# Other places for the weight loads of the slot experts in a fused convolution and expert kernel

## The chip, the core and the metric

The kernel runs on one core of a Trainium2 chip. The core has a matrix engine (TensorE, PE in the rows; PEld is its loading of the stationary operand), a vector engine (VectorE, DVE), a scalar engine (ScalarE, ACT), a general engine (GpSimd, POOL) and a sequencer that issues most transfers (SyncE, SP). Sixteen DMA engines move data between memory and the core's on-chip buffers. The metric is the device time in microseconds (us), as the median of several runs.

## What is computed

```python
# _attn_ref: softmax over 7 taps per head, then a causal 7-tap convolution whose weights differ by row and head
w = np.exp(weight_gen - weight_gen.max(-1)); w /= w.sum(-1)          # [4, 3584, 8, 7]
out = np.einsum('bshk,bskhg->bshg', w, x_unf)                        # x: [4, 3584, 192]
# _moe_ref: soft slots, 8 experts x 4 slots
logits = x @ phi                                                     # [14336, 32]
slot_input = softmax(logits, over rows).T @ x                        # [32, 192]
for e in range(8):
    slot_out[e] = np.maximum(slot_input[e] @ w1[e], 0.0) @ w2[e]     # w1 [192, 1024], w2 [1024, 192]
x = softmax(logits, over slots) @ slot_out
# _moe2_ref: each row goes to its best of 8 experts, scaled by two gates
...
```

The change concerns the weights `w1` and `w2` of `_moe_ref`, here called the slot experts' weights.

## The kernel before

The first stage, some 177 of 280 us, runs over 32 groups `g` of 112 rows in each of the 4 sequences. For each group SP loads rows of the input (`load_x`, line 318, tile x: one large and two small transfers) and normalised tap weights (`load_v`, line 300, tile vt: the same three), and VectorE (quarters q = 0 and 2) and GpSimd (q = 1 and 3) make banded matrices from vt (`band`, line 331). TensorE multiplies x by the bands (`conv`, line 352, into psA and psB), computes the slot logits (line 369) and turns the result (line 383); ScalarE copies between. A running softmax over the rows adds up the slot inputs (lines 393 to 454).

The tap weights pass through a softmax of their own, in six blocks: load (`w_load`, line 148, tile wg), maximum (line 157), subtraction, exponential, sum, normalisation (`w_rot`, line 209, tile vr), and a store to scratch memory vscr (`w_store`, line 214), out of which `load_v` reads. Blocks 0 to 2 are done in the prologue; block 3 is loaded there and finished in groups 1 to 4, block 4 runs in groups 2 to 11, block 5 in 9 to 20. So the vt load of a group waits for the store of its block.

The slot experts' weights are 24 transfers, three for each expert e: 512 KB of `w1` (w1a, line 277), the remaining 256 KB of `w1` (w1b, line 279) and 768 KB of `w2` (w2s, line 281). They have buffers of their own, so nothing has to be free first. Loop g of the groups 1 to 24 issues number g - 1, in the order expert by expert. Below, a0 is w1a of expert 0, b0 its w1b, w0 its w2s. They are used only after the groups: w1a and w1b in lines 787 and 789, w2s in line 803 (first four f blocks of experts 0 to 3, then of experts 4 to 7, then the other four).

SP issues all of these from one queue in the order of the program, and where a transfer has to wait, all behind it wait. Each transfer uses one of eight completion semaphores in turn, so that it also waits for the landing of the transfer eight places earlier. x has three buffers, so the x load in loop g (for group g + 2) waits for the matmuls of group g - 1; vt has four buffers.

After the groups a second softmax, over the slots, runs in four chunks on VectorE, ScalarE and GpSimd; its result is stored to scratch memory cscr (line 561) and loaded back turned (`load_c`, line 565, tile cT; two transfers a chunk). Chunks 0 and 1 are stored during the groups and loaded right after them; chunks 2 and 3 follow beside the slot experts. Their output (so, line 819) picks one expert, whose weights SP then loads (lines 842 and 844, tiles w1t and w2t). The last stage, from about 220 us, writes the output.

Of the kernel before, what the change touches and what calls it, by code (L numbers as in the profile page):

```python
# [57 lines left out]
def dram_ap(t, off, dims):  # L58
    return bass.AP(t.tensor, t.offset + off, [list(d) for d in dims])
# [3 lines left out]
def attn_moe_moe_kernel(ctx: ExitStack, tc: tile.TileContext, x, wgen, phi, mw1, mw2, w_gate, w_ogate, w1, w2, out, dbg=None):  # L63
# [147 lines left out]
    def w_store(i):  # L211
        rt, t0 = RTS[i], T0S[i]
        vr = pcs.pop(i)[2].rearrange("p t h k -> p (t h k)")
        nc.sync.dma_start(dram_ap(vscr, (t0 + PAD) * HK, [[rt * HK, 32], [SROW * HK, B], [1, rt * HK]]), vr[:, 0 : rt * HK])
# [19 lines left out]
    for v, i in ((mask_s[:, 0:BT], -PAD), (mask_s[0:HI, BT:], -PAD), (mask_s[HI:P, BT:], 0), (mask_h[HI:P], -HI)):  # L234
        n = v.shape[-1]
# [37 lines left out]
    def load_moe(i):  # L273
        e, k = divmod(i, 3)
        r0 = 64 * (e // 4)
        if k == 0:
            nc.sync.dma_start(w1a[:, e, :], mw1[e, 0:P, :])
        elif k == 1:
            nc.sync.dma_start(w1b[r0 : r0 + 64, e % 4, :], mw1[e, P:D, :])
        else:  # L280
            nc.sync.dma_start(w2s[:, e], mw2[e].rearrange("(c p) d -> p c d", p=P))


    vts, xts, bts, pss, aTs, ats, Ls, dTs, lps = {}, {}, {}, {}, {}, {}, {}, {}, {}
# [12 lines left out]
    def load_v(g):  # L297
        vts[g] = p2.tile([P, B, HK], F32, tag="vt", name=f"vt_{g}", bufs=4)
        for p, t, n, b in rows(g):
            nc.sync.dma_start(vts[g][p : p + n, b:], dram_ap(vscr, (b * SROW + g * BT + t + PAD) * HK, [[HK, n], [SROW * HK, B - b], [1, HK]]))  # L300
# [302 lines left out]
    w_rot(0, range(0, 6))  # L603
    w_rot(0, range(6, K), nc.gpsimd)
    w_store(0)
    nc.scalar.dma_start(dram_ap(vscr, 0, [[HK, PAD], [SROW * HK, B], [1, HK]]), zrow.unsqueeze(1).to_broadcast([PAD, B, HK]))
    load_v(0)
    load_v(1)
# [6 lines left out]
    def store_1():  # L615
        w_store(1)
        load_phi(4, H)
        load_v(2)
        load_v(3)
        w_load(3)  # L620

    start = dict(
        phi=lambda: load_phi(0, 4),
# [10 lines left out]
        st1=store_1,  # L634
# [11 lines left out]
            start[f"b{g}{q}"] = lambda g=g, q=q: band(g, q)  # L646
    for n in PRO.split():
        start[n]()
    if PS[3][1] < 0:
        w_max(3, 0, RH // 2)  # L650

# [4 lines left out]
    def do_steps(t):  # L656
        for f, a in wsteps.pop(t, []):
            f(*a)

    for g in range(NG):  # L660
        m, hf = divmod(g, 2)
        if 2 < g + 2 < NG:
            load_x(g + 2)
        if 3 < g + 3 < NG:
            load_v(g + 3)
        if 1 <= g <= NG:
            conv_out(g - 1)
        if SM and hf == 1 and m >= 1:
            soft_m(m - 1)
        last = g + 1 == NG or g == 0  # L670
        if not last:
            band(g + 1, 0)
            band(g + 1, 3)

        if hf == 1 and m >= 1:
            if not SM:
                soft_m(m - 1)
            soft_2(m - 1)

        if hf == 0 and m >= 2:  # L680
            soft_p(m - 2)
            soft_a(m - 2)
        conv(g, 0)
        conv(g, 1)
        if hf == 0 and m >= 1:
            scores(m - 1)
            soft_0(m - 1)
        conv(g, 2)
        conv(g, 3)
        xts.pop(g)  # L690
        if not last:
            band(g + 1, 1)
        do_steps(3 * g)
        if g >= 1:
            if hf == 1 and m >= 1 and g < NG - 1:
                soft_t(m - 1)
                soft_d(m - 1)
            turn(g - 1, 0)
            turn(g - 1, 1)
        if not last:  # L700
            band(g + 1, 2)
        if hf == 0 and m >= 1:
            soft_1(m - 1)
        do_steps(3 * g + 1)
        if 1 <= g <= 24:
            load_moe(g - 1)
        if g == 2:
            nc.sync.dma_start(wgt[:, :, 0:E], w_gate.rearrange("(c p) e -> p c e", p=HC))
            nc.sync.dma_start(wgt[:, :, E : 2 * E], w_ogate.rearrange("(c p) e -> p c e", p=HC))
        if g == 20:  # L710
            wstack.close()
            cstack = ctx.enter_context(ExitStack())
            cpl = pool(cstack, "pcs", 2, "right")
            nc.vector.tensor_tensor(sel, ident[:, 0:32], ident[:, 32:64], op=ALU.add)
            nc.vector.tensor_tensor(sel, sel, ident[:, 64:96], op=ALU.add)
            nc.vector.tensor_tensor(sel, sel, ident[:, 96:128], op=ALU.add)
            nc.vector.tensor_copy(sel4, sel.unsqueeze(1).to_broadcast([P, 4, NS]))

            wm = cpool.tile([HC, 1], F32, tag="wm", name="wm")
            nc.vector.tensor_reduce(wm, wgt.rearrange("p c e -> p (c e)"), axis=AX.X, op=ALU.max, apply_absolute_value=True)  # L720
            nc.gpsimd.affine_select(tri, ones1, pattern=[[1, P]], compare_op=ALU.is_ge, fill=0.0, base=0, channel_multiplier=-1)
        do_steps(3 * g + 2)
    if dbg is not None:
        nc.sync.dma_start(dbg["acc"], acc)
    tail()
    s1.close()


# [208 lines left out]
    g16 = fp.tile([P, NT, 2 * E + 1], F32, tag="g16", name="g16")  # L937
# [371 lines left out]
    def kappa():  # L1309
# [5 lines left out]
        a0=lambda: g_out(0), a1=lambda: g_out(1), t0=lambda: g_turn(0), t1=lambda: g_turn(1),  # L1315
# [121 lines left out]
```

## Time and profile before

| | |
|---|---|
| time, median of 3 runs | 283.66 us (283.58 to 284.75) |
| profiled execution, its own time | 281.31 us |
| its span, first to last instruction | 279.5 us |
| granted TensorE clock, mean | 0.939 |
| busy: PE, DVE, ACT, POOL | 75%, 72%, 55%, 52% of the span |
| moved by DMA | 54.79 MB, 196 GB/s mean |
| chain that ended last, by engine | PE 40%, DMA 27%, DVE 10%, issue 7%, ACT 6% |
| in it, largest single line | DMA x<-in_x_dram 14% |

Busy time is an average over stages with different limits, so it is read by stretches. The chain follows the work that ended last back from the end: at each step to what released it, or to the instruction before it on the same engine. "issue" is time in which an engine waited for nothing that the profile shows. The DMA share of a stretch is the mean share of time in which the sixteen DMA engines were busy. The clock of a stretch is given as a share of full speed (2.4 GHz; the lower level, 1.2 GHz, is 0.5).

### The profile page before, as it was taken

The page shows a single profiled execution, that of the slowest core. Times are in us where ns is not written, and L with a number is a line of the kernel's source. Part 1 is how long each engine was busy: PE and PEld are TensorE (multiplying, and loading weights), DVE is VectorE, ACT ScalarE, POOL GpSimd, SP SyncE. Part 2 cuts the span into 40 slices and gives each one's busy share as a digit, 9 for nine tenths or more (in the row PEclk, how much of TensorE's full clock was granted, in tenths as well). Part 3 has the DMA queues.
Part 4 walks back from the last instruction along what each step waited for, and adds up shares of the span by engine and source line. Part 5 has one row for each costly group of instructions (what it writes and reads, how often), then busy time and mean ns, then how long its engine had stood idle before and what let it go on. Part 6 is the DMA issues. An engine that isn't in the chain of part 4 may idle for free.

```text
span 279.5 us, 12314 instructions
## 1 busy us (share of the span) xinstructions
PE 210.7 (75%) x5188; PEld 168.7 (60%) x5188; DVE 200.0 (72%) x458; ACT 152.6 (55%) x408; POOL 146.1 (52%) x161
## 2 busy tenths in 40 slices
PE   0035496987878779695988789999869899999850
PEld 0034375765757566574767567736747688988750
DVE  2998899645797439569495486387857897988760
ACT  2112273463755576452658567626314598889750
POOL 8174695795728867484677798425202040513000
PEclk9999688698999999997999999999986999999995
DMA  6825689999898989796998871375599067667780
GB/s 202 180 64 178 207 225 272 274 225 234 222 280 258 228 213 255 178 234 177 264 262 207 219 166 54 72 161 116 135 276 198 7 203 243 220 192 232 226 268 17
DMA packets 64809, 54.79 MB, mean 196 GB/s; under 512 B 20399, under 2 KB 61227, under 8 KB 64747
## 3 DMA queue, kind: packets, MB, share of 16 engines
q1 hardware_dynamic: 64707, 53.92, 72.4%
q8 instruction: 43, 0.70, 1.1%
q14 instruction: 19, 0.16, 0.2%
q10 hardware_dynamic: 40, 0.01, 0.0%
HBM read 37.85 MB, written 16.06 MB: 193 GB/s over the span
## 4 chain that ended last, share of the span: by engine, by line
PE 40%; DMA 27%; DVE 10%; issue 7%; ACT 6%; SPq 1%; DVEq 0%; ACTq 0%
DMA x<-in_x_dram 14%; PE tp L383 7%; PE psA L352 7%; PE psB L352 5%; DMA out_dram<-ot 3%; DMA w2t<-in_moe_w_dram 3%; PE op L1382 3%; PE L L369 3%; DMA w2s<-in_moe_w_dram 2%; PE sp L444 2%; PE op L1385 2%; PE op L1384 2%; PE op L1383 2%; DMA vt<-vscr 2%; DMA vscr<-vr 2%
## 5 line engine op out<-in xcount | busy, mean ns | idle before, releaser
L331 POOL TENSOR_TENSOR bt<-vt,mask_s 128x448 f32<-128x448 f32 (+1 forms) x63 | 95.2, 1537 | 41.0 <-DMA vt<-vscr 27.3
L352 PE MATMUL psA<-bt,x 64*32 64x56 f32 (+1 forms) x1568 | 54.3, 246 | 27.9 <-issue 13.1
L331 DVE TENSOR_TENSOR bt<-vt,vbank 128x448 f32<-128x448 f32 x65 | 53.2, 832 | 28.1 <-DMA vt<-vscr 16.1
L352 PEld LDWEIGHTS psA<-bt,x 64*32 64x32 f32 (+1 forms) x1568 | 36.2, 114 | 41.0 <-issue 21.8
L352 PE MATMUL psB<-bt,x 64*32 64x56 f32 (+1 forms) x1568 | 54.7, 245 | 5.5 <-issue 5.5
L387 ACT ACTIVATE at<-tp 112x384 f32<-112x384 f32 x62 | 29.8, 492 | 28.2 <-PE tp L383 27.1
L383 PE MATMUL tp<-ident,aT 128*112 128x128 f32 x256 | 39.6, 291 | 1.4 <-DVE acc L454 0.9
L352 PEld LDWEIGHTS psB<-bt,x 64*32 64x32 f32 (+1 forms) x1568 | 36.7, 114 | 6.3 <-issue 6.3
L383 PEld LDWEIGHTS tp<-ident,aT 128*112 128x112 f32 x256 | 29.4, 141 | 6.4 <-ACT d L432 3.6
L1387 ACT ACTIVATE ot<-op,S 128x192 f32<-128x192 f32 x77 | 29.1, 431 | 5.0 <-DMA out_dram<-ot 1.7
L1382 PE MATMUL op<-wm,hi 128*128 128x192 f16 x112 | 27.5, 245 | 3.3 <-ACT ot L1387 1.9
L1385 PE MATMUL op<-Ml,cT 128*128 128x192 f16 x112 | 27.5, 246 | 0.2 <-DVE Ml L1306 0.2
L1383 PE MATMUL op<-wm,lo 128*128 128x192 f16 x112 | 27.5, 246 | 0.1
L1384 PE MATMUL op<-wm,hi 128*128 128x192 f16 x112 | 27.5, 246 | 0.1
L1076 DVE SCALAR_TENSOR_TENSOR lo<-hp,hi 128x512 f16<-128x512 f32 x28 | 19.1, 681 | 2.7 <-ACT hi L1075 2.6
L168 ACT ACTIVATE wg<-wg 128x952 f32<-128x952 f32 (+3 forms) x11 | 9.0, 829 | 19.8 <-DVE wg L164 9.0
L357 ACT ACTIVATE aT<-psA 128x224 f32<-128x224 f32 (+1 forms) x60 | 18.4, 361 | 1.5 <-PE psA L352 1.5
L357 ACT ACTIVATE aT<-psB 128x224 f32<-128x224 f32 (+1 forms) x60 | 19.0, 380 | 0.0
L1075 ACT ACTIVATE hi<-hp 128x512 f16<-128x512 f32 x28 | 16.8, 600 | 3.7 <-PE hp L1074 3.6
L369 PE MATMUL L<-aT,phi_p 128*32 128x112 f32 x512 | 17.0, 268 | 0.9 <-issue 0.6
L164 POOL TENSOR_TENSOR wg<-wg,mx 128x952 f32<-128x952 f32 (+3 forms) x9 | 13.6, 1527 | 6.0 <-DVE mx L157 6.0
L1383 PEld LDWEIGHTS <-lo 128*128 128x128 f16 x112 | 10.9, 97 | 8.1 <-DVE ot L1389 1.9
(265 smaller groups left out, 394.7 us busy)
## 6 DMA issues: line engine op xcount, KB each, us to landing
x<-in_x_dram SPq DMA_DIRECT2D x32, 336.0 KB
w2s<-in_moe_w_dram SPq DMA_DIRECT2D x8, 768.0 KB
out_dram<-ot SPq DMA_DIRECT2D x15, 384.0 KB
w1a<-in_moe_w_dram SPq DMA_DIRECT2D x8, 512.0 KB
cT<-cscr SPq DMA_DIRECT2D x8, 448.0 KB
vt<-vscr SPq DMA_DIRECT2D x32, 98.0 KB
out_dram<-ot SPq DMA_DIRECT2D x9, 288.0 KB
vscr<-vr SPq DMA_DIRECT2D x3, 784.0 KB
```

What stands on the lines that cost most here:

```text
L331: (nc.gpsimd if onp else nc.vector).tensor_tensor(bt.rearrange("p h (r k) -> p h r k", k=K), vt.unsqueeze(2).to_broadcast([n, H, w // K, K ...
L352: nc.tensor.matmul(out, xt[p, q * D + GR * h : q * D + GR * h + 32], bt[p, h, :], start=True, stop=True, tile_position=(HI * (r or 0), o))
L357: act = lambda o, i: nc.scalar.activation(o, i, AF.Copy)
L369: nc.tensor.matmul(Ls[m][32 * b : 32 * b + 32, o], phi_p[:, c, :], aTs[2 * m + q][:, c, b * BT : (b + 1) * BT], start=(c == 0), stop=(c == ...
L383: nc.tensor.transpose(tp[:, q, c, :], aTs[g][:, c, o : o + BT], ident)
L387: nc.scalar.activation(o, i, AF.Copy)
L1076: low = lambda: nc.vector.scalar_tensor_tensor(lo[:, f, :], hp, 0.0, hi[:, f, :], op0=ALU.max, op1=ALU.subtract)
L1382: nc.tensor.matmul(op, hi[:, 0, tok], wm2[:, 0, :], start=True, stop=False)
L1383: nc.tensor.matmul(op, lo[:, 0, tok], wm2[:, 0, :], start=False, stop=False)
L1384: nc.tensor.matmul(op, hi[:, 0, tok], wm2[:, 1, :], start=False, stop=False)
L1385: nc.tensor.matmul(op, cT[:, t * P : (t + 1) * P], Ml, start=False, stop=True)
L1387: nc.scalar.activation(ot[:, j, :], op, AF.Copy, scale=S0[:, t : t + 1])
```

## The change

The loop's `load_moe(g - 1)` goes, and a table names the place of each of the 24 transfers. Six go into the prologue: a0 behind the store of block 0, a1 behind the first four phi loads, and a2, b0, b1, a3 behind the load of block 3. The other w1 parts stand two or three loops apart. w0, w1 and w2 are issued in loops 19, 22 and 25, and w3 to w7 in loops 29 to 31. No transfer is added or removed, and no instruction of another engine changes its place.

```diff
+    MOE = dict(
+        st0="a0", phi="a1", st1="a2 b0 b1 a3", g4="b2", g6="a4", g8="b3", g10="a5", g11="b4", g13="a6", g14="b5", g16="a7", g17="b6", g19="w0",
+        g20="b7", g22="w1", g25="w2", g29="w3", g30="w4 w5", g31="w6 w7",
+    )
+
+    def load_moe_at(when):
+        for n in MOE.pop(when, "").split():
+            load_moe(3 * int(n[1]) + "abw".index(n[0]))
...
     w_store(0)
+    load_moe_at("st0")
...
         w_load(3)
+        load_moe_at("st1")
...
         start[n]()
+        if n == "phi":
+            load_moe_at(n)
...
         do_steps(3 * g + 1)
-        if 1 <= g <= 24:
-            load_moe(g - 1)
+        load_moe_at(f"g{g}")
```

SP's queue in the prologue, from the load of block 3 on (wg_3; vr_2 is the store of block 2, x4_0 the x load of group 3, vt_4 that of group 4). Before:

```order
L148 DMA wg_3_253<-in_weight_gen_dram 128x1x1904
L214 DMA vscr_62<-vr_2_274 32x4x784
L318 DMA x4_0_149<-in_x_dram 112x4x192
L318 DMA x4_0_149<-in_x_dram 8x4x192
L318 DMA x4_0_149<-in_x_dram 8x2x192
L300 DMA vt_4_363<-vscr_62 112x4x56
```

And now:

```order
L148 DMA wg_3_255<-in_weight_gen_dram 128x1x1904
L277 DMA w1a_142<-in_moe_w1_dram 128x1024
L279 DMA w1b_143<-in_moe_w1_dram 64x1024 x2
L277 DMA w1a_142<-in_moe_w1_dram 128x1024
L214 DMA vscr_62<-vr_2_280 32x4x784
L328 DMA x4_0_149<-in_x_dram 112x4x192
L328 DMA x4_0_149<-in_x_dram 8x4x192
L328 DMA x4_0_149<-in_x_dram 8x2x192
L310 DMA vt_4_369<-vscr_62 112x4x56
```

Four weight loads have come between the load of block 3 and the store of block 2.

SP's queue in loops 14 and 15, in the middle of the groups. Before:

```order
L279 DMA w1b_143<-in_moe_w1_dram 64x1024
L318 DMA x4_2_151<-in_x_dram 112x4x192
L318 DMA x4_2_151<-in_x_dram 8x4x192
L318 DMA x4_2_151<-in_x_dram 8x2x192
L300 DMA vt_18_1863<-vscr_62 112x4x56
L300 DMA vt_18_1863<-vscr_62 8x4x56
L300 DMA vt_18_1863<-vscr_62 8x2x56
L281 DMA w2s_144<-in_moe_w2_dram 128x8x192
L318 DMA x4_0_149<-in_x_dram 112x4x192
```

And now:

```order
L279 DMA w1b_143<-in_moe_w1_dram 64x1024
L328 DMA x4_2_151<-in_x_dram 112x4x192
L328 DMA x4_2_151<-in_x_dram 8x4x192
L328 DMA x4_2_151<-in_x_dram 8x2x192
L310 DMA vt_18_1862<-vscr_62 112x4x56
L310 DMA vt_18_1862<-vscr_62 8x4x56
L310 DMA vt_18_1862<-vscr_62 8x2x56
L328 DMA x4_0_149<-in_x_dram 112x4x192
```

The second weight between two groups' loads is gone; the w1b load ahead of them is now that of expert 5 instead of expert 4.

SP's queue from the last x load on (c2_1, c2_2 and c2_3 are chunks 1 to 3 of the softmax over the slots). Before:

```order
L318 DMA x4_1_150<-in_x_dram 8x2x192
L561 DMA cscr_63<-c2_1_3539 32x2x896 x4
L565 DMA cT_3729<-cscr_63 64x3584 x4
L561 DMA cscr_63<-c2_2_3822 32x2x896 x4
L561 DMA cscr_63<-c2_3_3855 32x2x896 x4
```

And now:

```order
L328 DMA x4_1_150<-in_x_dram 8x2x192
L281 DMA w2s_144<-in_moe_w2_dram 128x8x192
L571 DMA cscr_63<-c2_1_3535 32x2x896 x4
L281 DMA w2s_144<-in_moe_w2_dram 128x8x192 x4
L575 DMA cT_3729<-cscr_63 64x3584 x4
L571 DMA cscr_63<-c2_2_3822 32x2x896 x4
L571 DMA cscr_63<-c2_3_3855 32x2x896 x4
```

One second weight stands ahead of the stores of chunk 1, four behind them and ahead of the cT loads. In both programs the four stores of chunk 3 wait for the semaphores of the four cT loads.

## Rows read from the trace of the kernel before

**Rows 1.** Stretches: us, busy PE, PEld, DVE, ACT, POOL, clock, DMA share, GB/s

```profile
21.00:35.00 14.00, 6.82 (x265) 5.84 (x264) 12.26 (x25) 3.77 (x7) 7.94 (x7) 0.83 0.64 194
41.70:75.10 33.40, 26.70 (x782) 21.31 (x774) 21.95 (x42) 17.32 (x51) 23.49 (x16) 0.85 0.93 240
75.10:156.90 81.80, 65.45 (x2208) 52.41 (x2200) 57.08 (x111) 47.68 (x141) 55.66 (x37) 0.98 0.91 237
156.90:174.40 17.50, 15.45 (x516) 12.13 (x516) 12.21 (x18) 11.96 (x34) 14.66 (x11) 1.00 0.52 125
176.60:194.00 17.40, 16.48 (x228) 9.57 (x231) 12.10 (x28) 7.94 (x16) 6.12 (x6) 1.00 0.60 134
194.00:203.00 9.00, 7.77 (x129) 6.45 (x117) 8.08 (x22) 3.51 (x5) 2.35 (x3) 1.00 0.54 125
```

**Rows 2.** Stretches, the matmuls of line 352 alone: us, busy PE (count), PEld (count)

```profile
41.70:75.10 33.40, 12.99 (x576) 10.23 (x576) 0.85 0.93 240
75.10:156.90 81.80, 32.25 (x1632) 26.00 (x1632) 0.98 0.91 237
156.90:174.40 17.50, 8.02 (x384) 6.00 (x384) 1.00 0.52 125
```

**Rows 3.** Chain by line, 75 to 157; one piece (start, us); 41.7 to 75.1

```profile
by line: DMA x<-in_x_dram 46.8%; DMA w2s<-in_moe_w_dram 8.1%; DMA vt<-vscr 7.6%; PE psA L352 7.5%; DMA vscr<-vr 7.4%; PE psB L352 5.3%; PE tp L383 4.3%; issue 2.7%; DVE vr L209 2.1%; PE L L369 1.9%; PE sp L444 1.6%; SPq L300 1.5%; PE tl L42
...
91.31 6.67 DMA w2s<-in_moe_w_dram
...
by line: PE tp L383 23.8%; issue 19.6%; PE psA L352 15.7%; PE psB L352 11.6%; PE L L369 6.3%; PE sp L444 6.3%; ACT aT L357 5.9%; ACT wg L168 5.9%; PE tl L427 4.2%; ACT dT L415 1.1%; ACT at L387 0.2%
```

**Rows 4.** Waits (us, times, longest): four of 75.1 to 156.9; last, 41.7 to 75.1

```profile
POOL bt L331 <- DMA vt<-vscr: 14.9, 10, 3.7
POOL bt L331 <- PE psB L352: 12.0, 5, 6.2
...
PE psA L352 <- DMA x<-in_x_dram: 10.8, 7, 3.8
DVE bt L331 <- DMA vt<-vscr: 10.8, 6, 2.7
...
POOL bt L331 <- DMA vt<-vscr: 9.1, 5, 3.3
```

**Rows 5.** SP's issues in the prologue: start us, us of issue, line, tile, count

```profile
18.58 0.55 SPq L214 DMA_DIRECT2D vscr<-vr  x1
...
21.05 2.22 SPq L300 DMA_DIRECT2D vt<-vscr  x6
23.38 0.59 SPq L148 DMA_DIRECT2D wg<-in_weight_gen_dram  x1
27.36 0.52 SPq L214 DMA_DIRECT2D vscr<-vr  x1
...
30.84 1.09 SPq L300 DMA_DIRECT2D vt<-vscr  x3
```

**Rows 6.** VectorE in the prologue: start us, us; idle before in brackets

```profile
28.60 2.19 DVE L157 TENSOR_REDUCE mx<-wg 128x136 f32<-128x952 f32 x2 [1.27 <-DMA wg<-in_weight_gen_dram]
...
36.09 1.09 DVE L331 TENSOR_TENSOR bt<-vt,vbank 120x896 f32<-120x896 f32 x1
```

**Rows 7.** SP's issues after the groups

```profile
175.98 2.61 SPq L561 DMA_DIRECT2D cscr<-c  x4
182.64 2.37 SPq L565 DMA_DIRECT2D cT<-cscr  x4
194.43 4.68 SPq L561 DMA_DIRECT2D cscr<-c  x8
201.06 0.89 SPq L842 DMA_DIRECT2D w1t<-in_moe_w_dram  x2
```

**Rows 8.** TensorE and VectorE at the second weights' matmuls and their sum

```profile
192.36 4.11 PE L803 MATMUL sop<-w2s,hTz 128*32 128x192 f32 x96
...
197.46 0.41 DVE L819 TENSOR_SCALAR so<-sop,rden 128x192 f32<-128x192 f32 x1
```

More of the change, by code (lines that the diff above doesn't have):

```diff
@@ L725, in attn_moe_moe_kernel @@
     tail()
+    assert not MOE
     s1.close()
```

## The prediction

> **What bounds the kernel now.** I read the stretches first, then the pace of the groups, then the chain that ended last, then the waits. In the stretches the reader is to look at one column, the share of time in which the 16 DMA engines are busy: 0.93 from 41.7 to 75.1 us and 0.91 from 75.1 to 156.9, where TensorE, VectorE and GpSimd are busy for 65 to 80% of the time; then 0.52 from 156.9 to 174.4, where no slot weights are loaded any more [rows 1]. The pace: a group from the third on has 96 matmuls of line 352, so a count divided by 96 is a number of groups. 576 are 6 groups in 33.4 us (5.57 us each), 1632 are 17 groups in 81.8 us (4.81 each), and 384 are 4 groups in 17.5 us (4.37 each) [rows 2]. The same work goes at 4.37 us a group when the DMA engines are half idle. The chain says the same for the second stretch: from 75 to 157 us, 46.8% of it is the landing of x loads, and 8.1%, 7.6% and 7.4% are w2s, vt and vscr transfers. In the first stretch it lies on TensorE and on "issue", so transfers bound it less clearly there [rows 3]. Those who wait: GpSimd for vt 14.9 us in 10 waits, VectorE for vt 10.8 in 6, TensorE for x 10.8 in 7 in the second stretch, and GpSimd for vt 9.1 in 5 in the first [rows 4]. The waits overlap, so they are no sum.
>
> **The price of a load.** Busy 0.91 of the time the DMA engines moved 237 GB/s, busy 0.93 of it 240 [rows 1]: about 260 GB/s when fully busy. A second weight (768 KB, 786 kB in tens) costs 3.0 us of all 16 engines, a w1a part (512 KB) 2.0, a w1b part (256 KB) 1.0. That is an estimate from mean rates: the vt and x loads beside them come in smaller pieces, so the true price of a weight may be lower. The Trainium skill, page "DMA: Bandwidth & Descriptors", section Specifications, gives 358 GB/s as a core's limit from memory; by that the three would be 2.2, 1.5 and 0.7 us, and each relief below would shrink by a quarter. The rows show no stretch above 240, so I keep my prices.
>
> **Part 1, the second stretch (groups 10 to 26): gain.** Before, loops 10 to 24 issue five loads of each kind here: 5 x (3.0 + 2.0 + 1.0) = 30 us of DMA. After, there are three w1a, four w1b and three second weights: 6 + 4 + 9 = 19 us. So 11 us leave 0.91 x 81.8 = 74.4 us. If the pace followed the DMA work, 63.4 / 74.4 x 4.81 = 4.1 us a group, which is less than the 4.37 of the free stretch, so the engines would bind first. The bound from above is 17 x (4.81 - 4.37) = 7.5 us. Below it: at 4.37 the DMA engines are still busy for 63.4 of 74.3 us, 0.85, and three 3 us loads remain, each able to hold an x load back as in the 6.67 us piece of the chain [rows 3]. From below: 0, if what the x wait hides is another wait. I take two thirds, **-5.0 us**, nearer to the row of the free stretch.
>
> **Part 2, the first stretch (groups 4 to 9): gain.** Before, two w1a, two w1b and three second weights are issued here, the last at its end (12 to 15 us); after, one w1a and two w1b (4 us). 8 to 11 of 0.93 x 33.4 = 31 us go. The bound is 6 x (5.57 - 4.37) = 7.2 us, but the granted clock was 0.85 here [rows 1], part of it at the lower of the two levels (1.2 GHz), and two blocks of the softmax over the kernel's taps run on VectorE and GpSimd; the chain names TensorE first. What surely ends at a transfer is a part of GpSimd's 9.1 us. I take **-3.0 us**, with 0 and -7.2 as ends.
>
> **Part 3, the prologue: loss.** Six loads (four w1a, two w1b: 10 us of DMA) come earlier. The DMA engines had room, idle for 0.36 x 14 = 5.0 us from 21 to 35 [rows 1], but what stands behind the weights is urgent. a0 goes out while SP waits for the store of block 0, and has little behind it that is due soon: 0. a1 stands ahead of the store of block 1 (18.58); the vt loads of groups 2 and 3 wait for that store (21.05), and behind them stands the wg load of block 3 (23.38) [rows 5]. 0.4 us of issue and up to 2.0 of transfer make wg late by 1 to 2.4 us. VectorE waits for exactly that landing, 1.27 us before line 157 at 28.60 [rows 6], and is nearly always busy around it (12.3 of 14 us from 21 to 35, [rows 1]): I take +1.5. a2, b0, b1, a3 (6 us) stand ahead of the store of block 2 (27.36), for which SP's vt load of group 4 waited until 30.84 [rows 5]. The store then lands 4 to 6 us later. VectorE's bands of group 4 begin at 36.09 [rows 6]. Giving that vt load some 2.5 us (the next vt loads went out 2.47 us after the store at 18.58, [rows 5]), it was there by 33.4, so 2.7 us of slack plus the 1.5 just lost cover most of it; what sticks out is 0 to 1.8 us. I take +0.5. Sum **+2.0 us**; ends 0 (all of it runs where VectorE is the slower) and +5.
>
> **Part 4, the tail: nearly hidden.** w3 goes out in loop 29, and SP then waited until 175.98 for the stores of chunk 1 [rows 7]: hidden. w4 to w7 follow those stores, from 178.6 (175.98 + 2.61) on: 12 us of DMA, done at about 190.6, landed by 191 to 193. The matmuls that take experts 4 to 7 begin in the block at 192.36, and VectorE reaches their sum only at 197.46, about 1 us after their end at 196.47 [rows 8]: that us covers it. Behind the four stand the cT loads (issued at 182.64, [rows 7]). From 176.6 to 194 the DMA engines were idle for 0.40 x 17.4 = 7.0 us, from 194 to 203 for 0.46 x 9 = 4.1 [rows 1]; 12 us of new work fit by 203 with 0.9 us over. The order matters there: the four stores of chunk 3 reuse the semaphores of the four cT loads, before as after, so SP cannot pass them before the last cT load has landed, now at some 199 (12 less 7.0 is 5 us past 194), and the chosen expert's weights (201.06) stand behind those stores. I take **+0.5 us**; ends 0 and +3.
>
> **Sum.** -5.0 - 3.0 + 2.0 + 0.5 = -5.5 us. The profiled execution took 281.31 us (span 279.5), so 275.8 by its own time. The median of the runs, 283.66, is 2.35 above it; I set the sum against that median: 278.2 us.
>
> **Rivals.** *The engines set the pace.* If the groups of the two stretches are slow because GpSimd, VectorE and the clock make them so, the loads come earlier and nobody uses it: GpSimd also waits 12.0 us for psB in the second stretch, in the same answer as its vt wait [rows 4]. Then part 1 gives 2.5, part 2 nothing, the losses stay: 283.7 us. Against it: the 4.37 us of the free stretch, with the same work per group.
>
> *All of the relief arrives.* Both stretches go at 4.37: -7.5 - 7.2 + 2.5 = -12.2, 271.5 us. For it: fewer pauses of TensorE would also leave fewer stretches at the lower clock. Against it: the first stretch's chain is not on transfers.
>
> *Slower: the store of block 2 behind four weight loads.* If the whole 6 us reach the store, and the x load of group 3, queued behind it, is as late, then the 2.7 us of slack are used up and some 3.3 us plus the 1.5 us of wg fall on VectorE, 5 us in all, at the start, where nothing later waits on less. The kernel gets slower from the point where parts 1 and 2 together give less than 5.5 us: with 2.5 from part 1 alone the time is 283.66 + 5.0 + 0.5 - 2.5 = 286.7 us. For it: four loads stand in SP's order ahead of the store of line 214, which is due. Against it: the room of 5.0 us from 21 to 35 [rows 1]. The Trainium skill, same page, section "Queues, rings and completion order", says that each DMA engine takes descriptors in ring order; by that rule the store waits for all four loads, and this case's rows (a store at 27.36 that let vt go at 30.84 with the wg load still ahead of it) do not contradict it.
>
> That the change does not do what it says can be left out: SP's order shows the loads in their new places.
>
> **Chances.** Forecast 0.64, all of the relief 0.12, engines set the pace 0.13, slower 0.11. A measurement of this kernel tells about 0.5%, 1.4 us, from no change. Faster by more than that: 0.64 + 0.12 = 0.76; within it: 0.13; slower: 0.11. The range goes from 271.5 (full relief) to 284.0 (no relief): outside lie the slower case, half of the full one and a third of the no-relief one, 0.2 together. The forecast's own range, from its ends without the extremes, is 274 to 282.
>
> **What would show it.** Part 1: 1632 matmuls of line 352 in under 78 us, a DMA share near 0.85, and x loads with under 35% of the chain. Part 2: the 6 groups in about 30 us, GpSimd's vt wait well under 9 us. Part 3: VectorE's wait for wg before the 136-column maximum grown from 1.27 us to 2 to 3.5, and a new wait for vt at the first bands of group 4. Part 4: no TensorE wait for w2s over 1 us, and SP's load of the chosen expert within 1 us of its old place after the sum. I am wrong if the groups keep 4.8 us with the DMA share below 0.85 (engines), or if GpSimd or VectorE stands for over 4 us before group 4 (slower).

## The result, and the profile after

The changed kernel took 278.64 us (median of 4 runs, 275.54 to 287.76) against 284.16 for the kernel before in the same series; the ratio is 0.972, 95% interval 0.966 to 0.978. The forecast was 278.2. That agreement is not worth what it looks like. The comparison leaves out runs more than 1.5% above the fastest of their kernel, which kept two of these four (275.54 and 276.99) and keeps as few as 2 of 10 in the series below, so the ratio of the medians of all runs, here 0.981, is given beside it. The same kernel was therefore timed twice more, in 12 runs each, on two chips: 283.59 against 283.51 us (ratio 0.997, 0.992 to 1.002; by the medians 1.000), and 281.34 against 283.97 (0.983, 0.975 to 0.991; by the medians 0.991). Faster, then, in two of three series, by something between nothing and 2.8%; over both long series the medians are 282.77 us in 24 runs and 283.64 in 58 runs of the kernel before, 0.3% apart.

The rows below are of the first repetition's profiled execution (283.27 us); that of the first series took 287.76 us, the longest of its four runs, and serves only to show how far traces of one kernel differ. This execution's span is 2.0 us longer than that of the kernel before (279.5). The page, sections 1 and 4:

```profile
span 281.5 us, 12316 instructions
...
PE 213.6 (76%) x5188; PEld 172.1 (61%) x5188; DVE 201.3 (71%) x458; ACT 152.2 (54%) x408; POOL 145.7 (52%) x161
...
PE 46%; DMA 17%; DVE 10%; ACT 8%; issue 6%; SPq 6%; POOL 2%; ACTq 0%; DVEq 0%; POOLq 0%
```

Transfers have gone from 27% to 17% of the chain that ended last, TensorE from 40% to 46%, and SP's own queue (SPq) from 1% to 6%. So the weights did leave the place where they held the chain, and the span did not follow. Stretch by stretch (us of the stretch; busy PE, PEld, DVE, ACT, POOL with counts; clock; DMA share; GB/s), cut at the first conv matmul of groups 5, 10 and 27 and at the last of group 31. Before:

```profile
47.60:75.19 27.59, 23.00 (x639) 18.29 (x642) 16.14 (x25) 15.69 (x46) 20.85 (x14) 0.82 0.90 229
75.19:156.98 81.79, 65.36 (x2208) 52.37 (x2197) 56.99 (x111) 47.67 (x140) 55.74 (x37) 0.98 0.91 236
156.98:176.52 19.54, 17.57 (x613) 13.72 (x614) 12.21 (x18) 14.00 (x41) 16.70 (x12) 1.00 0.47 113
```

And now:

```profile
52.58:77.96 25.38, 20.78 (x638) 16.41 (x642) 18.17 (x32) 15.44 (x45) 22.07 (x15) 0.93 0.76 193
77.96:158.50 80.54, 68.07 (x2208) 55.53 (x2197) 59.78 (x112) 46.38 (x138) 56.10 (x38) 0.92 0.75 189
158.50:178.82 20.32, 17.51 (x614) 13.61 (x614) 11.59 (x18) 14.76 (x43) 16.01 (x11) 1.00 0.66 174
```

Read the first number of each row, where the stretch begins, and then its length. Group 5 begins 5.0 us later. Groups 5 to 9 give back 2.2 us, groups 10 to 26 only 1.25, although the DMA share there fell from 0.91 to 0.75. Groups 27 to 31 take 0.8 us more. In one table, with the start of the chosen expert's load (201.06 before, [rows 7], 204.53 after) as the end of the tail:

| step | forecast | this trace |
|---|---|---|
| prologue, to the start of group 5 | +2.0 | +5.0 |
| groups 5 to 9 (forecast: 4 to 9) | -3.0 | -2.2 |
| groups 10 to 26 | -5.0 | -1.3 |
| groups 27 to 31 | 0 | +0.8 |
| last group's end to the chosen expert's load | +0.5 | +1.2 |
| from there to the end | 0 | -1.5 |
| sum | -5.5 | +2.0 |

**What one trace can tell.** The last row is a warning: nothing after the chosen expert's load was edited, yet that stretch took 76.1 to 78.6 us in the five traces of before, this one, e1_late_only, e3_behind_store and f3_tail_spread. The groups scatter no less: groups 10 to 26 of this same kernel took 80.54 us here, 81.60 in the trace of the second repetition and 84.01 in that of the first series. A difference under some 2 to 3 us in one stretch of one trace therefore shows nothing by itself; whole kernels are compared by their series of runs. Of the kernel before there is one trace.

### The profile page after: what moved, and what is told of

It reads as the page before. It is cut to its first block, busy times and chain, and to the rows that moved or that the text cites. A ratio compares the mean times of both kernels' runs of the same rounds, so it can differ in the third digit from the quotient of the medians.

```text
span 286.0 us, 12316 instructions
## 1 busy us (share of the span) xinstructions
PE 214.2 (75%) x5188; PEld 170.7 (60%) x5188; DVE 201.3 (70%) x458; ACT 152.6 (53%) x408; POOL 146.0 (51%) x161
## 4 chain that ended last, share of the span: by engine, by line
PE 33%; DMA 26%; DVE 11%; ACT 7%; POOL 7%; SPq 6%; issue 6%; ACTq 0%; POOLq 0%; DVEq 0%
DMA vt<-vscr 6%; DMA vscr<-vr 6%; PE tp L393 5%; DMA w2s<-in_moe_w_dram 5%; DMA x<-in_x_dram 4%; POOL bt L341 4%; PE psA L362 3%; DVE vr L209 3%; DMA out_dram<-ot 3%; PE psB L362 3%; PE op L1396 3%; PE sp L454 2%; PE L L379 2%; PE op L1399 2%; PE op L1398 2%
## 5 line engine op out<-in xcount | busy, mean ns | idle before, releaser
L362 PE MATMUL psA<-bt,x 64*32 64x56 f32 (+1 forms) x1568 | 52.7, 246 | 24.9 <-issue 12.0
L362 PEld LDWEIGHTS psA<-bt,x 64*32 64x32 f32 (+1 forms) x1568 | 35.5, 114 | 38.7 <-issue 26.4
L362 PE MATMUL psB<-bt,x 64*32 64x56 f32 (+1 forms) x1568 | 53.6, 244 | 3.1 <-issue 2.9
L393 PE MATMUL tp<-ident,aT 128*112 128x128 f32 x256 | 41.1, 300 | 2.4 <-ACT at L397 1.2
L393 PEld LDWEIGHTS tp<-ident,aT 128*112 128x112 f32 x256 | 30.6, 145 | 7.4 <-ACT d L442 3.9
L379 PE MATMUL L<-aT,phi_p 128*32 128x112 f32 x512 | 18.1, 274 | 1.9 <-issue 1.6
L403 ACT ACTIVATE lall<-L 128x224 f32<-128x224 f32 x15 | 5.4, 358 | 26.0 <-PE L L379 26.0
```

The lines of the kernel that those rows point to most:

```text
L362: nc.tensor.matmul(out, xt[p, q * D + GR * h : q * D + GR * h + 32], bt[p, h, :], start=True, stop=True, tile_position=(HI * (r or 0), o))
L379: nc.tensor.matmul(Ls[m][32 * b : 32 * b + 32, o], phi_p[:, c, :], aTs[2 * m + q][:, c, b * BT : (b + 1) * BT], start=(c == 0), stop=(c == ...
L393: nc.tensor.transpose(tp[:, q, c, :], aTs[g][:, c, o : o + BT], ident)
```

## The experiments

All diffs are against the changed kernel; where only the table of places differs, the diff shows the table's entries that matter.

### The changed kernel again

> The changed kernel unaltered, for an undisturbed trace of it. The prediction's theory: 0.966 to 0.980 of the time before; groups 10 to 26 in under 78 us, VectorE waits 2 to 3.5 us for the wg landing of block 3, TensorE waits under 1 us for w2s in the tail. Rival (the tail is not hidden): TensorE waits over 2 us for w2s, and the chosen expert's load moves back by as much against the end of the groups.

283.59 us, ratio 0.997 (0.992 to 1.002): the expectation of the forecast fell on this chip, and what the trace shows at the start is the rival with the store of block 2. VectorE (start us, us; idle before in brackets):

```profile
30.19 2.19 DVE L157 TENSOR_REDUCE mx<-wg 128x136 f32<-128x952 f32 x2 [3.73 <-DMA wg<-in_weight_gen_dram]
...
43.19 1.09 DVE L341 TENSOR_TENSOR bt<-vt,vbank 120x896 f32<-120x896 f32 x1 [5.46 <-DMA vt<-vscr]
```

SP's issues (start us, us of issue):

```profile
28.44 0.59 SPq L277 DMA_DIRECT2D w1a<-in_moe_w_dram  x1
29.12 0.57 SPq L214 DMA_DIRECT2D vscr<-vr  x1
29.79 1.52 SPq L328 DMA_DIRECT2D x<-in_x_dram  x3
40.88 1.09 SPq L310 DMA_DIRECT2D vt<-vscr  x3
```

And the chain of that stretch has one piece

```profile
29.12 11.71 DMA vscr<-vr
```

The wait for wg grew from 1.27 us [rows 6] to 3.73. The store of block 2 goes out at 29.12 instead of 27.36 [rows 5] and lands 11.71 us later, so the vt load of group 4 leaves at 40.88 instead of 30.84, and VectorE, which went into the bands of group 4 at 36.09 with no wait [rows 6], now stands for 5.46 us. The four weights ahead of the store landed at 34.55, 35.98, 37.65 and 40.01, the store at 40.83 (last completion event of each): in the order of the queue. The Trainium skill, page "DMA: Bandwidth & Descriptors", section "Queues, rings and completion order", says that each DMA engine consumes descriptors in ring order; these five landings agree. It says too that completions need not come in the order of issue, and the trace of the kernel before has such a case: an x load of 24 KB issued at 39.31 landed at 45.04, ahead of the 336 KB one issued at 38.71 (45.81).

### The second weights late, nothing in the prologue

```diff
-        st0="a0", phi="a1", st1="a2 b0 b1 a3", g4="b2", g6="a4", ... g19="w0", ... g22="w1", g25="w2", g29="w3", g30="w4 w5", g31="w6 w7",
+        g1="a0", g2="b0", g4="a1", g5="b1", ... g19="a6 w0", g20="b6", g22="a7 w1", g23="b7", g25="w2", g29="w3", g30="w4 w5", g31="w6 w7",
```

> Only the second weights move (w0, w1, w2 to loops 19, 22, 25, w3 to w7 to 29 to 31); the w1a and w1b loads stand one by one in loops 1 to 23 as before, none in the prologue. Theory (the relief comes by volume of DMA, the prologue costs 2 us): 6 us of DMA leave the second stretch instead of 11, 9 leave the first: -3.0 - 3.0 + 0.5 = -5.5 us, a ratio of 0.98 like the whole change. Rival (the prologue costs 4 us or more): -7 us or better than the whole change, 0.972 or less. Rival (the early w1 parts bring most of the gain): 0.99 or more.

282.94 us, ratio 0.987 (0.980 to 0.993), 1.0% under the changed kernel on the same chip; but by the medians it is 0.998, 0.2% under the changed kernel (282.94 against 283.59). That it is faster than the changed kernel is therefore not shown. Its prologue is that of the kernel before (VectorE):

```profile
28.75 2.19 DVE L157 TENSOR_REDUCE mx<-wg 128x136 f32<-128x952 f32 x2 [1.39 <-DMA wg<-in_weight_gen_dram]
...
36.24 1.09 DVE L340 TENSOR_TENSOR bt<-vt,vbank 120x896 f32<-120x896 f32 x1
```

Group 5 begins at 47.27 (47.60 before, 52.58 in the changed kernel). Its groups 10 to 26, with first weights beside more of them and a DMA share of 0.81 instead of 0.75, are no slower than those of the changed kernel:

```profile
73.33:153.47 80.14, 67.16 (x2208) 53.56 (x2197) 57.44 (x112) 46.49 (x138) 56.11 (x38) 0.96 0.81 208
```

So nothing here shows a gain from loading six first weights early; whatever the change wins would come from the late second weights. The next run tests the early loads by themselves.

### The prologue loads alone

```diff
-        ... g6="a4", ... g19="w0", ... g22="w1", g25="w2", g29="w3", g30="w4 w5", g31="w6 w7",
+        ... g3="w0", g6="a4 w1", g9="w2", g12="w3", g15="w4", g18="w5", g21="w6", g24="w7",
```

> Only the w1a and w1b loads move (six in the prologue, the others further apart); the second weights stay in loops 3, 6, 9 to 24, none comes after the groups. Theory: prologue +2.0, first stretch -0.5, second stretch 5 us less DMA -2.0, tail 0: -0.5 us, 0.998. Rival (the prologue costs 4 us or more and is not won back): 1.007 or more. Rival (the early loads bring most of the gain): 0.985 or less.

285.57 us, ratio 1.007 (1.003 to 1.011), by the medians 1.007 as well: the early loads cost more than the thinner groups return, as the first rival said. With the run before, the two halves of the change give -1.3% and +0.7%, together -0.6%, beside -0.3% of the whole on the same chip; by the medians -0.2% and +0.7%, together +0.5%, beside 0.0%. Either way the early loads take away at least half of what the late ones give.

### The four loads behind the store of block 2

```diff
-        ... st1="a2 b0 b1 a3", ...
+        ... st2="a2 b0 b1 a3", ...
...
-        if n == "phi":
+        if n in ("phi", "st2"):
```

> The changed kernel, but a2, b0, b1, a3 stand behind the store of block 2 instead of ahead of it. Theory (wg is late through a1 alone, the store costs 0.5): 0.5 us less than the changed kernel, VectorE's wait for wg as in it. Rival (the four loads right behind the wg load slow its landing, since transfers in flight share the engines): VectorE's wait for wg falls by over 1.5 us, the time by 2 to 4 us. Second rival (the x and vt loads behind them are now late instead): no gain or a loss up to 3 us, with a wait for vt at the bands of groups 4 and 5.

281.06 us (4 runs), ratio 0.983 (0.973 to 0.993), by the medians 0.991. On this chip that is under the changed kernel (0.997 and 1.000), with intervals that just touch, and it is not because the start was mended. VectorE:

```profile
31.12 2.19 DVE L157 TENSOR_REDUCE mx<-wg 128x136 f32<-128x952 f32 x2 [3.74 <-DMA wg<-in_weight_gen_dram]
...
42.15 1.09 DVE L340 TENSOR_TENSOR bt<-vt,vbank 120x896 f32<-120x896 f32 x1 [3.50 <-PE psB L361]
```

The store now landed at 32.32, but the vt load of group 4, issued at 32.52, stood behind the same four weights and landed at 41.78. Group 5 began at 51.27, only 1.3 us earlier. The wait for wg is unchanged at 3.74 us, with the four loads now behind wg and the store: a0, a1 and the later issue of wg alone suffice for it. Of the rest, its groups 5 to 26, which this experiment did not aim at, are 3.4 us shorter than in the trace of the changed kernel and its groups 27 to 31 are 2.8 us longer, so what won its time is open. Groups 10 to 26:

```profile
75.15:153.80 78.65, 65.70 (x2207) 52.34 (x2196) 59.99 (x112) 46.26 (x138) 58.16 (x40) 0.98 0.76 198
```

### The changed kernel a third time

> The changed kernel once more, unaltered, because its first two measurements disagree (0.972 and 0.997 of the time before). If the change is worth what was forecast (-5.5 us), the ratio comes out near 0.98. If the prologue takes nearly all that the groups give back (group 5 began 5.0 us later than before in the trace of the first repetition, 52.58 against 47.60, and the groups from there on took 2.7 us less, 126.2 against 128.9), it comes out at 0.99 to 1.00. The trace should again show the store of block 2 landing near 40 us (30.8 before) and the fifth group beginning 4 to 5 us late; if it does not, the prologue's loss is itself a matter of chance.

281.34 us, ratio 0.983 (0.975 to 0.991), on another chip. Its trace again has group 5 late, at 51.40, and that of the first series has it at 52.49. So the prologue's loss is no matter of chance, and the total comes out between 0.97 and 1.00 all the same. Its groups 10 to 26 gained almost nothing on the 81.79 us before:

```profile
75.05:156.65 81.60, 67.36 (x2207) 54.38 (x2196) 59.91 (x112) 46.27 (x138) 57.84 (x39) 0.94 0.72 188
```

### Spread evenly

```diff
+        g1="a0", g2="b0", g3="w0", g4="a1", g6="b1", g7="w1", g8="a2", g9="b2", g11="w2", ... g26="w6", g27="a7", g28="b7", g29="w7",
```

> No load in the prologue; the 24 loads in the old order, expert by expert, but spread over loops 1 to 29 (five in every six loops) instead of one in each of loops 1 to 24. Theory of the transfers (the DMA work beside a group sets its pace): loops 1 to 24 carry 20 loads instead of 24, some 8 us of DMA less, and the free stretch behind them has room for it; groups 5 to 31 take 122 to 125 us instead of 128.9, the prologue and the tail are as before, and the ratio is 0.98 to 0.99. Theory of the engines: the groups keep their pace, ratio 1.00, within 0.4%.

284.41 us, against 283.97 before; ratio 0.991 (0.982 to 1.000), by the medians 1.002. That is no gain that can be told from none, and 3 us more than the changed kernel on the same chip (281.34). Its one trace has 131.4 us for groups 5 to 31, against 128.9 before and the 122 to 125 of the theory: 20 loads instead of 24 in loops 1 to 24 do not by themselves make 2%.

### No weights beside the groups

```diff
+        g31="a0 a1 a2 a3 a4 a5 a6 a7 b0 b1 b2 b3 b4 b5 b6 b7 w0 w1 w2 w3 w4 w5 w6 w7",
```

> All 24 loads stand in loop 31, so no group has a weight load beside it and the slot experts wait for their weights: only the time up to the end of the groups is read. Theory of the transfers: the groups from 5 on go at the 4.37 us of the free stretch before, 27 of them in 118 us instead of 128.9, and the DMA share falls to about 0.5. Theory of the engines: they still take 125 us or more, because VectorE, GpSimd and TensorE set the pace. Everything that can be won in parts 1 and 2 by moving weights lies between the two.

The whole takes 303.22 us, since the slot experts wait for their weights; the groups show the floor. Groups 10 to 26, and their chain:

```profile
70.61:146.04 75.43, 64.40 (x2208) 52.56 (x2197) 58.33 (x112) 46.32 (x138) 56.29 (x38) 0.98 0.54 144
```

```profile
by line: PE tp L392 18.9%; PE psA L361 12.7%; PE psB L361 9.4%; PE sp L453 9.4%; PE L L378 8.7%; issue 7.1%; ACT aT L366 6.7%; DVE vr L209 5.0%; ACT at L396 4.5%; PE tl L436 3.2%; ACT dT L424 3.1%; ACT wg L168 2.5%; DVE sel L726 1.8%; ACT T
```

Groups 5 to 31 took 119.1 us (45.57 to 164.66) against 128.9 before. So, by these two traces, 9.8 us is all that taking weights out of these groups can give, 6.4 of it in groups 10 to 26, at 4.44 us a group. The transfer theory's 118 us was nearly right.

The loads, one behind the other, also test the price: 24 of them, 12.58 MB, from the first issue at 166.81 to the last landing at 215.0, are 261 GB/s, where 260 was estimated. But that agreement is one of means. Three stretches of it, in which w1a, w1b and w2s landed in turn:

```profile
174.96:178.80 3.84, 3.73 (x6) 0.54 (x6) 3.19 (x4) 0.00 (x0) 2.06 (x2) 0.62 1.03 418
184.27:193.50 9.23, 4.95 (x7) 0.68 (x8) 0.00 (x0) 0.00 (x0) 0.00 (x0) 0.52 1.07 214
193.50:210.40 16.90, 11.41 (x72) 4.67 (x70) 4.71 (x8) 5.59 (x7) 2.81 (x2) 0.76 1.12 328
```

With the DMA engines busy throughout they moved 418 GB/s of w1a, 214 of w1b and 328 of w2s: in the middle of each run of loads, one w1a landed every 1.28 us, one w1b every 1.25 and one w2s every 2.41, where the forecast had 2.0, 1.0 and 3.0. A price by the byte does not hold from one shape of load to another. The rate of 358 GB/s, by which the prediction also priced the loads, was exceeded in the first of these stretches.

### The last second weights one by one

```diff
-        ... g25="w2", g29="w3", g30="w4 w5", g31="w6 w7",
+        ... g25="w2", g26="w3", g27="w4", g28="w5", g29="w6", g30="w7",
```

Otherwise as the variant without prologue loads.

> As the variant without prologue loads (first weights one by one in loops 1 to 23, second weights from loop 19 on), but w3 to w7 go out one each in loops 26 to 30 instead of in 29 to 31. If the burst of four second weights behind the last groups is what delays the chosen expert's weights (VectorE's sum 21.1 us after the last matmul of the groups there, against 20.9 before and 22.1 in the changed kernel), the tail comes back to 20.9 and the ratio is that of the variant (0.987) or up to 0.5% lower. If the loads beside groups 26 to 30 cost as much as the ones of 10 to 24 did (up to 3 us each at the DMA engines), the groups end 2 to 5 us later and the ratio is 0.99 to 1.00.

281.77 us, ratio 0.994 (0.989 to 1.000), by the medians 0.992. The tail is as before (the last group's end to the chosen expert's load 24.55 us, before 24.54), but groups 27 to 31 took 23.45 us instead of 19.54. The second expectation fits: beside the last groups these loads cost 3.6 us by the end of the groups (177.76 against 174.14 in the variant with the burst), and the tail gives back 0.5.

### Only second weights, only first weights, halves

Three looks at the same bytes at the same places: 768 KB in each of loops 3, 6, ... 24, everything else in loop 31. First as w2s, then as w1a and w1b together, then as w2s in halves with the other half one loop later:

```diff
+        g3="w0", g6="w1", g9="w2", ... g24="w7", g31="a0 a1 ... b7",
```

```diff
+        g3="a0 b0", g6="a1 b1", g9="a2 b2", ... g24="a7 b7", g31="w0 w1 ... w7",
```

```diff
-            nc.sync.dma_start(w2s[:, e], mw2[e].rearrange("(c p) d -> p c d", p=P))
+            nc.sync.dma_start(w2s[:, e, 0:4], mw2[e, 0 : 4 * P].rearrange("(c p) d -> p c d", p=P))
+    def load_w2_rest(e):
+        nc.sync.dma_start(w2s[:, e, 4:8], mw2[e, 4 * P : 8 * P].rearrange("(c p) d -> p c d", p=P))
...
         load_moe_at(f"g{g}")
+        if 4 <= g <= 25 and g % 3 == 1:
+            load_w2_rest(g // 3 - 1)
```

> Beside the groups only the eight second weights (768 KB each), one in each of loops 3, 6, ... 24; all first weights wait for loop 31. Read from the start of group 5 to that of group 27 alone: 109.4 us before, 100.5 with no weights in the groups, 105 to 107 with three second weights and all the first ones (variant without prologue loads). If only the DMA work counts (the forecast's price by the byte), this variant and the next, with the same bytes at the same places, come out within 1.5 us of each other, near 104. If it is the second weights that cost (a burst of 768 KB ahead of an x load), this one takes 106 us or more.

> Beside the groups only the first weights, both parts of an expert (512 + 256 KB) in each of loops 3, 6, ... 24, the same 768 KB at the same places as the second weights of the variant beside it; all second weights wait for loop 31. Read from group 5 to group 27: near 104 us if only the bytes count; 101 to 102.5, close to the 100.5 with no weights at all, if the second weights are what costs.

> As the variant with the second weights alone, but each in two halves of 384 KB, the first in loops 3, 6, ... 24 and the other one loop later: the same bytes, half the size in front of any one x load. If the size of the burst matters (an x load behind a second weight landed 7 to 8.6 us after its issue, behind a first weight's small part some 4, with none 3.4), groups 5 to 27 take 2 us or more less than with whole second weights; if only the bytes count, the same within 1.5 us.

Groups 10 to 26 of the three, in this order:

```profile
70.80:152.52 81.72, 67.84 (x2207) 54.14 (x2196) 59.07 (x112) 46.59 (x138) 58.14 (x40) 0.94 0.75 198
```

```profile
70.45:150.34 79.89, 67.84 (x2208) 54.74 (x2197) 59.93 (x112) 46.42 (x138) 56.29 (x38) 0.94 0.75 191
```

```profile
69.94:147.69 77.75, 66.23 (x2207) 53.83 (x2197) 61.55 (x112) 46.44 (x138) 57.80 (x39) 0.96 0.75 198
```

From group 5 to group 27 they took 106.5, 105.2 and 102.1 us, against 100.5 with none. The first two lie within 1.5 us of each other, as for a price by the byte, though both above the 104 expected; the first also meets the mark of the other reading (106 or more), which the second does not (101 to 102.5). The halves, with the same DMA share of 0.75, are 4.4 us under the whole loads, which speaks against the share of busy DMA as what sets the pace. One thing that differs is how long the large x load right behind a weight takes from issue to landing: 6.8 us on average behind a whole second weight (7 of them), 5.4 behind two first weights, 5.2 behind a half (15), 4.3 to 4.6 in the loops without one. It does not explain the three: behind two first weights x landed almost as soon as behind a half, and those groups took 3.1 us more. Part of the 4.4 us is the clock: it was 0.96 instead of 0.94, and TensorE's same matmuls were 1.6 us shorter. These are single traces, and the scatter between traces of one kernel is almost as large, so the effect of the halves is not shown.

### A version from what was learnt

The second weights in halves, nothing in the prologue, one load a loop, the last three halves in loop 31:

```diff
-        e, k = divmod(i, 3)
+        e, k = divmod(i, 4)
...
-            nc.sync.dma_start(w2s[:, e], mw2[e].rearrange("(c p) d -> p c d", p=P))
+            c0, c1 = (0, 4) if k == 2 else (4, 8)
+            nc.sync.dma_start(w2s[:, e, c0:c1], mw2[e, c0 * P : c1 * P].rearrange("(c p) d -> p c d", p=P))
...
+        g1="a0", g2="b0", g3="w0", g4="v0", g5="a1", ... g25="a6", g26="b6", g27="a7", g28="b7", g29="w6", g31="v6 w7 v7",
...
-            load_moe(3 * int(n[1]) + "abw".index(n[0]))
+            load_moe(4 * int(n[1]) + "abwv".index(n[0]))
```

> A version made from what the runs showed: nothing in the prologue, the second weights in two halves of 384 KB, and of the 32 loads one in each of loops 1 to 29 (expert by expert), the last three halves in loop 31. If the size of what stands ahead of an x load sets the cost (7 whole second weights cost groups 5 to 27 some 6.1 us over the 100.5 with none, 7 pairs of halves 1.7), groups 5 to 27 take 103.5 to 105.5 us here against 109.4 before, the prologue is as before (group 5 at 46 to 47.5), the tail as before, and the ratio is 0.975 to 0.985. If the bytes alone count, it behaves like the variant with whole loads spread evenly over loops 1 to 29 (109.4 us; ratio 0.991): 0.99 to 1.00.

280.54 us against 284.11, ratio 0.984 (0.975 to 0.992), by the medians 0.987. It beats the kernel before, but its interval covers those of the changed kernel's second repetition (0.983), of the variant without prologue loads (0.987) and of the one with the loads behind the store (0.983). Its one trace (281.46 us, 0.3% above the median of its runs) does not bear out the halves. Groups 5 to 26 took 109.4 us (46.52 to 155.88), the figure that the expectation gives for a price by the bytes alone, that of the kernel before (109.4), and not 103.5 to 105.5. Groups 10 to 26:

```profile
73.44:155.88 82.44, 67.89 (x2207) 54.80 (x2196) 59.23 (x112) 46.47 (x138) 57.79 (x39) 0.94 0.83 213
```

Where this version wins its time is open.

## Why the prediction came out as it did

**The number was right in the first series, the sum behind it was not.** Part 1 and part 3 were both mis-sized, against the kernel. The traced execution gives +2.0 us where the sum has -5.5; the medians of the two long series give 0 and -2.6. That 278.2 and 278.64 agree is luck, owed to the scatter of a kernel whose own runs lie between 275.5 and 287.8 us, a scatter far above the 0.5% that I had taken a measurement to tell from no change.

**Part 3, the prologue: the wrong end of its range.** The term was +2.0 with +5 as its end; it measured +5.0 at group 5, +3.8 in the second repetition's trace. (Cut at group 4, as the forecast was, it is +6.3 here, beyond that end, and +2.4 there, so the table is cut where the traces agree better.) The step that failed is "the store then lands 4 to 6 us later", which became 10 (40.83 against some 30.8). I had counted the four loads' own 6 us. But wg was issued 1.65 us later (25.03 instead of 23.38, [rows 5]) and landed at 30.17, and from there to the landing of the last of the four, at 40.01, it took 9.8 us, while the engines moved no more than this:

```profile
30.17:34.55 4.38, 1.06 (x24) 1.09 (x28) 4.36 (x5) 0.74 (x1) 2.62 (x2) 0.55 1.03 225
34.55:40.01 5.46, 4.10 (x120) 3.27 (x112) 2.68 (x5) 4.12 (x11) 4.04 (x3) 0.74 0.81 221
```

The store landed 0.8 us behind the last of them. The 5.0 us of DMA room between 21 and 35 us [rows 1] that I held against this rival were real, but they did not help a store that stood behind the four loads in one queue. The term for wg, +1.5, was right: VectorE began line 157 at 30.19 instead of 28.60. The mark I had set, VectorE standing for over 4 us before group 4, came true (5.46). So the rival's mechanism and its 5 us were right; that the kernel gets slower by it was wrong, as the groups gave some of it back.

**Part 2: right.** The six groups 4 to 9 took 30.0 us (47.99 to 77.96; said: about 30; 31.0 in the second repetition's trace), and GpSimd's wait for vt in them is 3.0 us in 2 waits instead of 9.1 in 5 [rows 4]. How much of this is the relief and how much is groups that began late and found their blocks ready is not told apart: without any weights, groups 5 to 9 took 25.04 us, hardly less than the 25.38 here.

**Part 1: the step "I take two thirds".** The bound was good (7.5 us from [rows 2]; the floor run gives 6.4). The removal of transfers from the chain was good too: x loads fell from 46.8% of it [rows 3] to 7.3% (said: under 35%), and TensorE's wait for x from 10.8 us [rows 4] to under 0.3. The chain of groups 10 to 26 now:

```profile
by line: PE tp L393 21.0%; PE psA L362 15.0%; PE psB L362 11.0%; PE sp L454 10.0%; issue 9.1%; PE L L379 8.0%; DMA x<-in_x_dram 7.3%; DVE vr L209 4.7%; PE tl L437 4.0%; ACT aT L367 3.8%; ACT at L397 2.9%; DVE sel L728 2.4%; ACT dT L425 2.0%
```

But the pace was 4.74 us a group instead of under 4.6 (4.80 in the second repetition's trace), with the DMA share at 0.75 (0.72 there), well below the 0.85 forecast: what I had named as the sign of the rival *the engines set the pace*. Two candidates for what took the place of the x wait show in this trace. GpSimd still waits as long for its tap weights:

```profile
POOL bt L341 <- DMA vt<-vscr: 14.2, 8, 4.9
```

(14.9 in 10 before, [rows 4]; 9.0 in 5 with no weights at all.) But in the second repetition's trace that wait is 8.2 us in 6, and the stretch was no shorter, so this wait alone does not hold the pace. And TensorE, on which the chain now lies, was slower at the same work: 2208 matmuls took 68.07 us against 65.36, at a mean granted clock of 0.92 against 0.98, that is, with more time at 1.2 instead of 2.4 GHz. So of the 4.0 us by which its idle time in the stretch fell (81.79 - 65.36 = 16.4 us before, 80.54 - 68.07 = 12.5 now) the slower matmuls took back 2.7; in the second repetition's trace they took back 2.0 of 2.2. At one place where the clock fell, TensorE was busy for only 2.12 of 5 us (131 to 136), and the clock of the next 5 us, in which it was busy throughout, was 0.62:

```profile
131.00:136.00 5.00, 2.12 (x19) 1.94 (x10) 4.93 (x9) 1.51 (x4) 1.60 (x1) 0.70 1.00 259
136.00:141.00 5.00, 5.00 (x146) 4.03 (x144) 2.96 (x5) 1.86 (x7) 4.00 (x3) 0.62 0.46 113
```

That this clock belongs to the change is not shown: the variant with the loads behind the store had 0.98 in its groups 10 to 26 with the same loads there, and took 78.65 us, 3.1 less than before. Nor is it known how the kernel before scatters, of which the one trace has 0.98; eleven of the other thirteen traces lie below that here. So the relief of part 1 measured 0.2 and 1.3 us in the two repetitions' traces and 3.1 in that variant, where I had 5, and why the rest of the floor's 6.4 did not arrive is in part open.

**Part 4: the right place, too small.** The burst lands after it is wanted. TensorE and SP (as above) in the first repetition:

```profile
196.78 4.09 PE L817 MATMUL sop<-w2s,hTz 128*32 128x192 f32 x90 [1.59 <-DMA w2s<-in_moe_w_dram]
```

```profile
181.38 5.55 SPq L281 DMA_DIRECT2D w2s<-in_moe_w_dram  x4
187.11 4.54 SPq L575 DMA_DIRECT2D cT<-cscr  x4
196.71 6.38 SPq L571 DMA_DIRECT2D cscr<-c  x8
204.53 0.90 SPq L856 DMA_DIRECT2D w1t<-in_moe_w_dram  x2
```

The four loads were issued at 181.38, right behind the stores of chunk 1, and the last landed at 196.74, 15.4 us later, where I had 191 to 193. The wait for w2s is over the 1 us that I had set as the mark. The cT loads landed by 202.77, not by some 199: I had counted 5 us of DMA work past 194 as 5 us of time, although the row that I used has the engines busy for 0.54 of it. The chosen expert's load kept its distance from the sum (3.6 us before and after), so SP's order did not hold it up. The tail lost 1.2 us here and 2.9 in the second repetition's trace, the end of my range. What I left out altogether is that second weights beside groups 27 to 31 may slow these: they took 3.9 us more than before where five stood there, at a DMA share of 1.01; here, with w2 in loop 25 and w3 in loop 29, +0.8, within the scatter (18.6 to 20.2 us in traces with no whole weight there), and between +1.1 and +3.6 in the other traces with the same places.

**What stays open.** No run of the changed kernel of 275 to 278 us was traced, so which stretch such a run wins can't be said. Nor is it settled why the two long series of the same kernel differ (1.000 and 0.991 of before by their medians): they ran on different chips, and nothing here tells chip from chance. Whether a version without prologue loads really beats the changed kernel rests on one chip (0.987 against 0.997 with intervals that just touch, 0.998 against 1.000 by the medians).

## What to carry to other kernels

A transfer's share of busy DMA time is not what it costs: seven times 768 KB, some 21 us of DMA by the forecast's price, cost 22 groups 1.7 to 6.1 us in three single traces. Before pricing relief, run the loop with the transfers taken out; that floor (9.8 us here) is the most that moving them can give, and the part that arrived was smaller: from group 5 on 2.7 us in the first repetition's trace and 1.1 in the second's. Free DMA time in a stretch is no reason to put a large load ahead of a store that others wait for in the same queue: count the store behind everything issued before it, to the last landing.

## What the runs showed of the hardware

The scatter was larger than the three first runs of the kernel before (283.58 to 284.75 us) suggested: over the two long series its runs lie between 280.2 and 288.1 us, and those of the changed kernel between 275.5 and 286.7. Four runs could give 0.972 where twelve gave 0.997. The second surprise is the store of block 2, 392 KB: 3.4 us from issue to landing in the prologue before, 11.7 behind four weight loads; the 8.3 us more exceed the 6 us at which the forecast priced those loads. The third is how far the rate of busy DMA engines depends on the load: 418 GB/s for w1a and 214 for w1b, in one queue within 20 us.
